# A planned attention-and-MLP kernel: landing times of the inputs, order of the waits, and thresholds per half block

## The chip, the cores and the metric

The kernel runs on one core of one Trainium2 chip. The core has five engines that work at the same time: TensorE (PE in the profile; its weight loads are shown apart as PEld), VectorE (DVE), ScalarE (ACT), GpSimd (POOL) and SyncE (SP), which here only issues transfers. Data lie in SBUF (128 partitions), matrix products in PSUM (8 banks of 128 x 512 float32), inputs and the output in HBM. The metric is the device time of one execution in microseconds (us), the median of several runs, lower is better.

## The reference, cut to what matters

S = 2048 rows, D = 640, H = 32 heads of Dh = 20, F = 1536. There is one key head and one value head for all 32 query heads.

```python
xn = layernorm(x)                       # over D, eps 1e-5
q = (xn @ wq) as (H, S, Dh); k = xn @ wk; v = xn @ wv      # k, v: (S, Dh)
p = softmax(q @ k.T * Dh ** -0.5)       # 32 x 2048 x 2048
a = concat_h(p @ v) @ wo                # (S, D)
h = relu(xn @ w1 + b1) ** 2             # (S, F)
out = x + a + (h @ w2 + b2)
```

All inputs are bfloat16. The 32 x 2048 x 2048 exponentials are most of the work outside TensorE.

## The kernel before, in words

**Blocks, tiles, units.** The queries are cut in 4 chunks of 512 (`QC`), the heads in 8 groups of 4 (`G`), which makes 32 *blocks*. A block goes over 16 key *tiles* of 128 keys. A tile has 4 *units*, one per head: a 128 x 512 piece of scores. The first two blocks run interleaved, four key tiles of each at a time, as the keys become ready.

**Two ways to the exponential.** PE computes two to four units at once, one per group of 32 array rows (`S_QK`, `qk_ins`, L1100); such a *batch* writes up to four PSUM banks. Most units go to ACT, two or three per instruction (`S_EXP`, L1280), which writes bfloat16 exponentials into a ring `PT`. The tiles called D (`S_D`, `dtiles`) go to DVE instead: `S_P1` (L1377) makes from each unit an integer whose bits are a coarse exponential, and three *phases* with added offsets (`S_PH` on DVE, L1398, or in pieces on POOL, `S_PHP`, L1460) refine it. A D tile costs PE four groups of products with the values instead of one (`PVblk`, L1567: itself and three phases). So work can be moved between ACT on one side and DVE, POOL and PE on the other, tile by tile.

**The rest.** `u_KT`, `u_V` and `u_QP` make keys, values and queries from the normalised and transposed input (L732, L791); `u_FFN` (L732, then L888 on DVE and a square on POOL, L896) and `u_OUT`, `u_PA`, `u_PB`, `u_P1`, `u_PX`, `u_PF` make the MLP and the output. They are queued as `units` by a block position at which each may start (`FAT`, `FSTEP` for the MLP) and are taken up by `S_MISC`, and at the start by two more such streams, between the attention batches.

**The planner.** No order is written by hand. `Sched.run` simulates the five engines with a fixed duration for each request; of the requests that can start at the same time on an engine it takes that with the smallest priority number (batches 0, P1 2, PV 1 or 0.8, phases 4, keys 1.5, values 2). Thresholds looked up by block, `plan(name)` at L1078, decide how many units a batch takes, when a D tile is opened, which bank a side job takes and so on. What comes out is one fixed instruction list per engine, executed in order. A mistaken duration therefore costs nothing in the simulation, but on the chip it leaves an engine standing at an instruction whose input is late, with later ones behind it.

**The start.** SP issues `x` in five parts (`x_dma`: row tiles 0-1, 2-3, 4-7, 8-11, 12-15) with `wq` after the third; ACT issues `wk` and `wv`. The planner believes in the landing times `xland` and those in the `dma` calls (L556 to L569). DVE computes the statistics of a row tile (`stats`, L634, L636), ACT 1/sqrt for four row tiles at once (`rst`, L644, L648), then a row tile is normalised (`xnorm`, L662 on DVE or POOL; row tile 3 on ACT, L664 after L653). Row tiles 0 to 3 are transposed on PE (L721) and copied out (`evac_te`, L676, L677); row tiles 4 to 15 are transposed by DMAs on the SP queue (`turn`, L682), about 1.3 us of issue each. Before that PE runs 22 warm-up products (L604) and four filler groups (L1497).

**Waits.** `resolve` finds for each operation the semaphores it must wait on, one counter per engine and one per transfer chain; `emit` asks for them one after the other before the operation. In the program as built, the one asked for first is carried by the operation's own first instruction; all others become wait instructions in front of it in the engine's queue. Before the change the order is that in which the dependencies were collected:

```python
            for s_, v_ in wd.values():
                e.wait_ge(s_, v_)
```

## Time and profile before

| | |
|---|---|
| median of 3 runs (lowest, highest) | 708.11 us (707.29, 708.21) |
| the profiled execution | 707.32 us, span 705.5 us |
| PE, DVE, ACT, POOL busy | 687.5, 667.7, 680.1, 426.3 us |
| first and last exponential on ACT | start 14.91 us, end 691.2 us |
| exponentials on ACT | 607 of two units, 82 of three |
| granted TensorE clock | 1.0 throughout |

The span is the time from the first to the last instruction; 1.8 us lie around it. PE, DVE and ACT are each busy for about 95% or more, so a shortage on one of them is hidden from the totals: the profile must be read by stretches, and by what ended each idle time. "A <- B" in the list of waits says that A's engine stood idle until B was done.

### The profile page before, as it was taken

To read this page: it belongs to the slowest core of one execution; us is meant where nothing else is said; L and a number is where in the kernel's file an instruction comes from. 1 tells how busy PE (TensorE), PEld (TensorE's weight loads), DVE (VectorE), ACT (ScalarE), POOL (GpSimd) and SP (SyncE) were. 2 spreads that over 40 slices of the span, in tenths; PEclk is the share of its full clock that TensorE was granted. 3 is DMA by queue.
4 is the path that set the end of the run, shared out by engine and by line. 5 is a ranking of instruction groups with operands and counts; after the bars stand their busy time and mean duration, and the time that the engine had idled before them with its cause. 6 is when DMAs were issued, how large, how long until landed. Compare 5 with 4: busy or idle time off the path is not lost.

```text
span 705.5 us, 23364 instructions
## 1 busy us (share of the span) xinstructions
PE 687.5 (97%) x9874; PEld 221.9 (31%) x9874; DVE 667.7 (95%) x1145; ACT 680.1 (96%) x708; POOL 426.3 (60%) x696
## 2 busy tenths in 40 slices
PE   8899999999999999999999999999999999999997
PEld 4232222222223333332223333333222333333335
DVE  6978999999999999999999999999999999999974
ACT  5999999999999999999999999999999999999991
POOL 2547667767665666666766666666676656566400
PEclk9999999999999999999999999999999999999999
DMA  6476111011100111111100121111110101111101
GB/s 199 67 189 184 37 21 30 14 21 29 26 17 17 35 38 31 45 22 38 34 14 14 25 49 41 26 39 32 30 26 18 26 20 41 26 34 39 35 2 40
DMA packets 37955, 29.47 MB, mean 42 GB/s; under 512 B 20218, under 2 KB 33499, under 8 KB 37851
## 3 DMA queue, kind: packets, MB, share of 16 engines
q1 hardware_dynamic: 36539, 27.92, 16.6%
q8 instruction: 79, 1.29, 0.8%
q10 hardware_dynamic: 1312, 0.05, 0.1%
q14 instruction: 25, 0.20, 0.1%
HBM read 10.87 MB, written 2.62 MB: 19 GB/s over the span
## 4 chain that ended last, share of the span: by engine, by line
PE 66%; DVE 29%; DMA 2%; issue 1%; ACT 1%; POOL 1%; SPq 0%; DVEq 0%
PE ps L1567 24%; PE ps L1100 22%; PE ps L732 20%; DVE pbx L1377 15%; DVE pbx L1398 9%; DVE hT_tmp L888 2%; DMA pbx<-in_A_x_dram 1%; ACT PT L1280 1%; DMA xnT<-big 1%; DVE big L662 1%; POOL pbx L1460 0%; DVE stats L634 0%; DVE Tn L1612 0%; DVE out_sb L943 0%; DVE qpk L843 0%
## 5 line engine op out<-in xcount | busy, mean ns | idle before, releaser
L1280 ACT ACTIVATE PT<-ps 128x1024 bf16<-128x1024 f32 (+1 forms) x689 | 672.7, 1097 | 3.8 <-PE ps L1100 3.3
L1460 POOL TENSOR_SCALAR pbx<-pbx 128x576 int16<-128x576 uint16 (+13 forms) x518 | 317.8, 635 | 176.4 <-DVE pbx L1398 169.7
L1377 DVE TENSOR_SCALAR pbx<-ps 128x512 int16<-128x512 f32 x576 | 381.6, 689 | 12.8 <-PE ps L1100 11.5
L1100 PE MATMUL ps<-qT,kT 20*128 20x512 bf16 x2048 | 268.7, 384 | 5.4 <-DVE pbx L1377 1.8
L1398 DVE TENSOR_SCALAR pbx<-pbx 128x2048 int16<-128x2048 int16 x308 | 212.7, 710 | 0.4
L1567 PE MATMUL ps<-pbx,vp 128*32 128x512 bf16 x1764 | 162.4, 383 | 1.8 <-DVE pbx L1398 1.4
L1100 PEld LDWEIGHTS ps<-qT,kT 20*128 20x128 bf16 x2048 | 68.5, 91 | 262.4 <-ACT PT L1280 189.7
L1567 PE MATMUL ps<-PT,vx 128*32 128x512 bf16 x1460 | 142.3, 384 | 1.8 <-ACT PT L1280 1.5
L732 PE MATMUL ps<-w_sb,big 128*32 128x320 bf16 x1536 | 82.1, 302 | 0.0
L732 PE MATMUL ps<-xnT,w_sb 128*32 128x512 bf16 x960 | 78.1, 383 | 0.1
L896 POOL TENSOR_TENSOR big<-hT_tmp 128x288 bf16<-128x288 bf16 (+5 forms) x88 | 56.1, 654 | 27.0 <-DVE pbx L1398 27.0
L1567 PEld LDWEIGHTS ps<-pbx,vp 128*32 128x32 bf16 x1764 | 43.5, 95 | 51.7 <-issue 34.4
L1567 PE MATMUL ps<-pbx,vx 128*32 128x512 bf16 x588 | 57.9, 384 | 1.6 <-DVE pbx L1377 0.9
L1567 PEld LDWEIGHTS ps<-PT,vx 128*32 128x32 bf16 x1460 | 37.6, 94 | 49.5 <-issue 37.6
L1628 POOL TENSOR_TENSOR OTs<-Tn,Rb 128x224 bf16<-128x224 f32 (+5 forms) x42 | 32.8, 782 | 20.3 <-DVE pbx L1398 20.3
L732 PEld LDWEIGHTS ps<-w_sb,big 128*32 128x32 bf16 x1536 | 32.6, 95 | 29.9 <-issue 22.2
L888 DVE TENSOR_SCALAR hT_tmp<-ps,b1col 128x512 bf16<-128x512 f32 x48 | 35.4, 737 | 0.7 <-PE ps L732 0.4
L732 PE MATMUL ps<-wo_p,OTp 120*32 120x320 bf16 (+1 forms) x640 | 34.2, 302 | 0.1
L732 PE MATMUL ps<-xnT,wq_sb 128*32 128x512 bf16 (+2 forms) x435 | 33.8, 373 | 0.0
L732 PEld LDWEIGHTS ps<-xnT,w_sb 128*32 128x32 bf16 x960 | 19.2, 94 | 26.9 <-issue 20.2
L1567 PEld LDWEIGHTS ps<-pbx,vx 128*32 128x32 bf16 x588 | 15.3, 94 | 19.9 <-issue 10.9
L1612 DVE COPY Tn<-ps 128x512 f32<-128x512 f32 x29 | 19.6, 677 | 0.2 <-PE ps L1567 0.2
(75 smaller groups left out, 181.3 us busy)
## 6 DMA issues: line engine op xcount, KB each, us to landing
Rb<-Rr SPq DMA_DIRECT2D x29, 256.0 KB
w_sb<-in_B_w_dram SPq DMA_DIRECT2D x2, 1920.0 KB
xres<-in_A_x_dram SPq DMA_DIRECT2D x16, 160.0 KB, 3.0
out_dram<-out_sb SPq DMA_DIRECT2D x16, 160.0 KB
qT<-qpk SPq DMA_DIRECT2D x105, 20.0 KB
pbx<-in_A_x_dram SPq DMA_DIRECT2D x3, 640.0 KB
OTp<-OTs SPq DMA_DIRECT2D x96, 20.0 KB
wq_sb<-in_A_wq_dram SPq DMA_DIRECT2D x1, 800.0 KB
```

Of the source, the lines that this page charges most:

```text
L662: fn = lambda e: e.tensor_scalar(out=xn_sb[:, st, :], in0=x_sb[:, st, :], scalar1=mean, scalar2=rstd[:, st:st + 1], op0=ALU.subtract, op1= ...
L732: return lambda e: e.matmul(ps[32 * j:32 * j + m, b_[0], 0:n], Lj, R, start=first, stop=last, tile_position=(0, 32 * j))
L888: v = yield Req(("dve", 658.0, 742.0, [lambda e: e.tensor_scalar(out=hT_tmp[:, k, :], in0=ps[:, b_[0], :], scalar1=b1col[:, f:f + 1], scal ...
L896: w = yield from pieces(512, 139.0, 1.7, lambda c0, c1: (lambda e: e.tensor_tensor(out=h2T[:, qc % 2, f, c0:c1], in0=hT_tmp[:, k, c0:c1], ...
L1100: ins.append(lambda e, i=i, b=b, t=t, h=h: e.matmul(ps[:, i, :], kT[32 * h:32 * h + DH, t * 128:(t + 1) * 128], qT[32 * h:32 * h + DH, b % ...
L1280: op = yield Req(("act", d_, d_ + 107.0, [lambda e, slot=slot, n=n, src=src: e.activation(out=PT[:, slot:slot + n, :], in_=ps[:, src, :], ...
L1377: return Req(("dve", d_, d_ + 82.0, [lambda e: e.tensor_scalar(out=PB[:, k, hsl, :], in0=ps[:, bk:bk + np_, :], scalar1=OFFS, scalar2=0.0, ...
L1398: return Req(("dve", 600.0, 684.0, [lambda e: e.tensor_scalar(out=PB[:, k, :, :], in0=PB[:, s, :, :], scalar1=PH_D[j], scalar2=None, op0=A ...
L1460: return lambda e: e.tensor_scalar(out=PB[:, k, :, :].rearrange("p h n -> p (h n)")[:, c0:c1], in0=PBU[:, s, :, :].rearrange("p h n -> p ( ...
L1567: ins = [(lambda e, h=h, first=first, last=last: e.matmul(ps[32 * h:32 * h + 32, bk, :], lhs, rhs[h], start=first, stop=last, tile_positio ...
L1612: v = yield Req(("dve", 600.0, 682.0, [lambda e: e.tensor_copy(out=Tn[:, tb, :], in_=ps[:, pvb, :])]), (lambda: None if oldt() is None els ...
L1628: w = yield from pieces(512, 138.0, 2.14, lambda c0, c1: (lambda e: e.tensor_tensor(out=dst[:, c0:c1], in0=Tn[:, tb, c0:c1], in1=Rb[:, a, ...
```

## The change

Four things are changed; no operation is added to or taken from the computation as such, but the planner's result, and so the whole order, may come out different.

1. **Landing times.** `xland` and the times of `wq`, `wk`, `wv` are set to other values. Row tiles 4-7 of `x`, for example, are now taken to land at 8.7 us instead of 6.7.
2. **Priorities at the start.** The projections of keys and values for chunks 1 to 3 get priority 0.9 instead of 1.5 and 2, which places them before ordinary PV groups (1); the copy of the values out of PSUM gets 14 for these chunks.
3. **Waits.** The semaphores of an operation are sorted by the planned completion of what they wait for, latest first. The latest therefore rides on the operation's own instruction, and the earlier ones are asked for in front of it.
4. **Thresholds.** The table `PLAN` has a row per half block (64) instead of one per block (32); four constants become columns of it (`give`, `await_`, `miscw`, `php`), and many values are different. The start positions of the MLP groups are changed: chunks 2 and 3 may start one block earlier (12 and 20 instead of 13 and 21) with a step of 0.36 instead of 0.33.

Against the row of the same block before, 58 of the 64 rows differ in at least one of the thirteen columns: 38 in `hungw`, 29 in `lead`, 27 in `ringhi`, 13 in `await_` (150 ns instead of 60 in 11 of them, 0 in 2), 9 in `miscw`, 8 in `give`, 6 in `php`.

```diff
-FAT = (1.0, 4.8, 13.0, 21.0)
-FSTEP = (0.3, 0.34, 0.33, 0.33)
+FAT = (1.2, 4.6, 12.0, 20.0)
+FSTEP = (0.28, 0.36, 0.36, 0.36)
...
+VPR, KPR, VEPR = 0.9, 0.9, 14.0
...
-GIVE = 3
...
+PSEG = 2
-PLAN_KEYS = ('lead', 'hungw', 'dstarv', 'clt', 'broken', 'p1tol', 'ringhi', 'miscr', 'mshift')
+PLAN_KEYS = ('lead', 'hungw', 'dstarv', 'clt', 'broken', 'p1tol', 'ringhi', 'miscr', 'mshift', 'give', 'await_', 'miscw', 'php')
...
-    (650.0, 3000.0, 600.0, 6000.0, 300.0, 900.0, 12, 2, 0.0),
-    (650.0, 3500.0, 600.0, 4500.0, 0.0, 900.0, 12, 2, 0.0),
+    (580.0, 3500.0, 600.0, 6000.0, 300.0, 900.0, 12, 2, 0.0, 3, 60.0, 300.0, 4.0),
+    (580.0, 3500.0, 300.0, 6000.0, 0.0, 900.0, 15, 2, 0.0, 3, 60.0, 300.0, 4.0),
+    (650.0, 4000.0, 600.0, 6000.0, 300.0, 900.0, 12, 2, 0.0, 3, 60.0, 300.0, 4.0),
+    (650.0, 3500.0, 600.0, 6000.0, 300.0, 900.0, 12, 2, 0.0, 3, 60.0, 600.0, 4.0),
...
-                    wd[d.sem.name] = (d.sem, d.val)
-            for s_, v_ in wd.values():
+                    wd[d.sem.name] = (d.sem, d.val, d.done)
+            for s_, v_, _ in sorted(wd.values(), key=lambda w: -w[2]):
                 e.wait_ge(s_, v_)
...
-        xland = [3700.0, 4600.0, 6700.0, 11000.0, 12900.0]
+        xland = [4000.0, 4850.0, 8700.0, 12000.0, 15000.0]
...
-        dma("sp", "wq", lambda e: e.dma_start(wq_sb[:], A_wq.rearrange("(dt p) n -> p dt n", p=128)), [], 8900.0)
+        dma("sp", "wq", lambda e: e.dma_start(wq_sb[:], A_wq.rearrange("(dt p) n -> p dt n", p=128)), [], 9800.0)
-        dma("act", "wk", lambda e: e.dma_start(wk_c[:], A_wk.rearrange("(dt p) d -> p dt d", p=128)), (lambda: get("tab")), 5000.0)
-        dma("act", "wv", lambda e: e.dma_start(wv_c[:], A_wv.rearrange("(dt p) d -> p dt d", p=128)), (lambda: get("tab")), 5500.0)
+        dma("act", "wk", lambda e: e.dma_start(wk_c[:], A_wk.rearrange("(dt p) d -> p dt d", p=128)), (lambda: get("tab")), 6300.0)
+        dma("act", "wv", lambda e: e.dma_start(wv_c[:], A_wv.rearrange("(dt p) d -> p dt d", p=128)), (lambda: get("tab")), 11000.0)
...
-            v0 = yield Req(("dve", 150.0, 230.0, [...]), [v], 10 + 4 * c, f"VE{c}")
+            v0 = yield Req(("dve", 150.0, 230.0, [...]), [v], 10 + 4 * c if c == 0 else VEPR, f"VE{c}")
...
-            return PLAN[min(NBLK - 1, int(pos()))][name]
+            return PLAN[min(NBLK * PSEG - 1, int(pos() * PSEG))][name]
...
-                    nd_ok = min(GIVE - (nd[0] - nd[1]), DMAXR)
+                    nd_ok = min(plan("give") - (nd[0] - nd[1]), DMAXR)
...
-                    free = [x for x in pool if freeat(x) <= t + AWAIT]
+                    free = [x for x in pool if freeat(x) <= t + plan("await_")]
...
-            return (min(fb, key=apart), sorted(freeat(x) for x in fb)[n] - MISCW) if len(fb) > n else None
+            return (min(fb, key=apart), sorted(freeat(x) for x in fb)[n] - plan("miscw")) if len(fb) > n else None
...
-... [acc[-1]] + pbres[k].last, 4 if left_ns(b) > URGN else 0.8, "PH", port=True)
+... [acc[-1]] + pbres[k].last, plan("php") if left_ns(b) > URGN else 0.8, "PH", port=True)
...
-            U(-3 + 0.1 * c + 0.05, f"KT{c}", ..., lambda b_, c=c: u_KT(c, b_, 1.5))
-            U(-3 + 0.1 * c + 0.06, f"V{c}", ..., lambda b_, c=c: u_V(c, b_, 2))
+            U(-3 + 0.1 * c + 0.05, f"KT{c}", ..., lambda b_, c=c: u_KT(c, b_, KPR))
+            U(-3 + 0.1 * c + 0.06, f"V{c}", ..., lambda b_, c=c: u_V(c, b_, VPR))
```

## The prediction

> **What bounds the kernel now.** I read the totals of the page, then the windows by stage, then what was waited for, then the first 15 us engine by engine. The totals say that three engines are full together:

> ```profile
> span 705.5 us, 23364 instructions
> PE 687.5 (97%) x9874; PEld 221.9 (31%) x9874; DVE 667.7 (95%) x1145; ACT 680.1 (96%) x708; POOL 426.3 (60%) x696
> ```

> The windows (PE, PEld, DVE, ACT and POOL busy) say which of them gives way where:

> ```profile
> 66.00:220.00 154.00, 148.09 (x1935) 42.62 (x1939) 153.46 (x253) 153.53 (x154) 104.22 (x157) 1.00 0.13 27
> 220.00:690.00 470.00, 467.98 (x6840) 149.80 (x6842) 454.06 (x757) 469.20 (x485) 291.05 (x480) 1.00 0.13 30
> ...
> 41.00:60.00 19.00, 18.46 (x242) 5.46 (x242) 13.48 (x23) 17.99 (x20) 9.48 (x15) 1.00 0.86 250
> 690.00:705.00 15.00, 11.62 (x336) 8.52 (x327) 6.78 (x18) 1.23 (x2) 0.00 (x0) 1.00 0.14 47
> ```

> From 66 to 220 us DVE and ACT have under 0.6 us of idle time and PE has 5.9; from 220 to 690 PE and ACT are full. The tail after the last exponential is a stream of PE products, 10 us long. What is left to gain is the first 66 us, short stalls, and the number of operations. The first input stall is a segment of the chain that ends last (its piece in the first 20 us), and then appears on DVE, ACT and PE:

> ```profile
> 1.82 6.92 DMA pbx<-in_A_x_dram
> ...
> 8.77 0.89 DVE stats L634 x2
> ...
> 9.75 0.92 ACT big L664
> ```
> ```profile
> 7.21 0.20 ACT L648 ACTIVATE rstd<-vtmp 128x4 f32<-128x4 f32 x1
> 9.75 0.92 ACT L664 ACTIVATE big<-pbx,nmr,rstd 128x640 bf16<-128x640 bf16 x1 [2.33 <-DVE nmr L653]
> ...
> 14.91 1.02 ACT L1280 ACTIVATE PT<-ps 128x1024 bf16<-128x1024 f32 x1 [0.57 <-PE ps L1100]
> ```
> ```profile
> 8.24 1.05 PE L1497 MATMUL ps<-hT_tmp,ones_bf 128*32 128x512 bf16 x16
> 10.12 0.45 PE L721 MATMUL ps<-ident,big 128*128 128x128 bf16 x5 [0.84 <-DVE big L662]
> ...
> 12.64 1.26 PE L732 MATMUL ps<-xnT,wq_sb 128*20 128x256 bf16 x40
> ```

> The reader should see that 1/sqrt is ready at 7.41 us, but DVE, in its fixed order, first takes the statistics of row tile 4, whose input lands at 8.74; nothing of row tiles 0 to 3 is normalised until 9.57. Last, the list of waits between 66 and 690 us (total, times, longest):

> ```profile
> PEld ps L1100 <- DVE pbx L1377: 12.1, 32, 0.4
> ...
> DVE pbx L1377 <- PE ps L1100: 6.8, 22, 0.8
> ```

> **Part A, landing times.** The semaphore records of the trace end at 4.07, 4.94, 8.74, 13.35 and 14.99 us for the five parts of x, 9.89 for wk, 11.44 for wq and 12.57 for wv. With 8.7 us for part three, the planner has the four normalisations (DVE starts 0.36 apart) ready at 7.4 and the statistics not before 8.8, so it turns their order round. The DVE gap of 1.81 us (6.96 to 8.77) is then used. The way to the first exponential gains less: PE is busy with warm-up and fillers until 9.29, so the first transposition moves from 10.12 to about 9.3 (0.83); its copies no longer queue behind L664 on ACT, so the first keys move from 12.09 to about 10.7, after wk; the queries move from 12.64 to no earlier than 11.44, where wq lands. From the queries on the chain is the same. The gain is between 0.83 and 1.2 us; I take 1.1, nearest to the wq row. The floor is 0, if the start is paid back later (a rival). The transfers are issued as before, in the same order, so SP pays nothing; the transposing DMAs move with their row tiles. The later figures for wk, wv and wq hold nothing up: keys and queries came after them anyway, and V starts at 14.81.

> **Part B, order of the waits.** I set each two-semaphore batch beside what released it in the trace's records. Where the later release had been asked for second, and is thus a wait instruction of its own, the batch starts 0.147 us after it ended, in 37 cases between 60 and 680 us, nearly always the same; where it had been asked for first, as little as 0.056 to 0.064. So 0.087 us is paid 37 times, 3.2 us of PE. Ten of these lie before 220 us, where PE has room. After 220, what a stall cost beyond the usual spacing (0.32 us from a batch's predecessor to it) is often less than 0.087, on average 0.06: 27 x 0.06 = 1.6 us. I take 1.3 and keep 0 and 3.2. Two-semaphore waits on DVE had the latest first in nearly all cases; POOL has some that turn round, and waited 155 us for DVE phases anyway, so nothing there; if that cover went, 15 x 0.09 = 1.3 us. What is queued behind a waiting batch is PE's PV and MLP groups, and ACT waits for it only when its two pending batches are used up. It can cost something where the planned latest is not the real one: in 44 of 448 two-semaphore batches, 0.087 each, 3.8 us if all of those were stalled, but only 9 of the 61 late ones were.

> [...]

> **Part C, priorities of keys and values.** Chunk 2's keys take from 37.95 to 40.1 on PE, five groups between batches and PV; then DVE copies them (0.75 at 40.61) and ACT stands idle for 0.93 us; 0.55 and 0.23 more at 25.6 and 29.1 hang on chunk 1. Groups of 0.22 us in a row would need 1.1 instead of 2.15 us. Of the 1.7 us of ACT idle time at most the first 0.93 is PE's order; the 0.55 is a PE stall on a transposing DMA. The work put back is PV, whose results nothing needs then. DVE has 5.5 us idle between 41 and 60. A D tile costs DVE 4 x 0.598 + 2.1 x 0.602 = 3.65 us (start to start, 2.1 of three phases on DVE: 308 for 147 tiles) and relieves ACT of 4 x 0.4525 = 1.81; so 1 us of DVE time is worth (1/3.65) / (1/3.65 + 1/1.81) = 0.33 us of time. Bounds 0 and 1.7 + 1.8 = 3.5; I take 0.5, half of the 0.93, since the DVE copy stays. VEPR places the value copies later on DVE: 0.15 each, with PV behind them; nothing.

> **Part D, thresholds per half block, and the MLP's starts.** These do no work themselves; they change which bank or batch is taken. From 66 to 690 DVE idles 16.5 us in the windows above, 6.7 of them in the last 8 us, where no D tile is left to make; of the other 9.8, 6.8 are waits for batches: x 0.33 = 2.2 us if all of it went. The other coin is PE: a batch costs 0.321 + 0.321 - 0.216 = 0.43 us (to it, from it, less what two neighbouring groups are apart anyway), and there are 689 (607 + 82 exponentials). A wider `await_` (150 ns in 11 half blocks) lets a unit join whose bank is free 90 ns later, and DVE's waits are mostly 0.1 to 0.4 us. Moving MLP groups a block forward moves 0.66 us of DVE each and changes no sum. Ends: 10 batches less or more, -4.3 to +4.3. I take -0.8, about a third of the DVE row's 2.2.

> **Sum.** 1.1 + 1.3 + 0.5 + 0.8 = 3.7 off the profiled 707.32 gives 703.6. That execution lies 0.8 below the median 708.11 and near the lowest of the three, so for a median I add half: 704.0. 0.2% is 1.4 us, about what a measurement of this kernel can tell from no change.

> **Rivals.** (1) The new plan makes more batches. The bound after 220 us is PE, which cannot hide 0.43 us each; the gains A to C of 2.9 us are used up at 7 more than 689, and 15 more cost 6.5 us: 708.1 - 2.9 + 6.5 = 711.7, slower from 11 on. For it: 58 of 64 rows differ, and `give` 2 or `hungw` 2600 in single half blocks make narrower batches. Against: in each column most rows hold the value that was the commonest before (`lead` 650 in 41 of 64, `give` 3 in 56). 22 in 100. (2) The start's gain is lost again at the keys of chunks 2 and 3: ACT comes 1.1 us earlier and waits 1.1 longer at 40.9, because the statistics of row tiles 8 to 15 and twelve transposing DMAs of 1.3 us on SP stand before them. Then C goes too, D comes out at nothing, and 708.1 - 1.3 = 706.8, no change. For it: that wait exists. Against: DVE itself gains the same 1.1 us. 12 in 100. (3) Ten batches fewer, or DVE's idle time in the first 66 us filled: 704.0 - 3.5 = 700.5. For it: 2.97 units per batch of four possible ones. Against: POOL and banks limit D. 24 in 100.

> **Numbers.** The forecast (702 to 706.5) has 42 in 100, rivals 22, 12 and 24. Faster by over 0.2%: 42 + 24 = 66; within: 12; slower: 22. The range leaves out 1 in 10 on each side: from 699.0, below rival 3, to 710.0, inside rival 1.

> **What would show it.** A: L662 starts by 7.7 us instead of 9.63, the first exponential at 13.8. B: no batch starts 0.147 us after its release. C: the 0.93 us before the exponential at 41.85 shrinks. D: count the exponentials and batches, and PE's busy time from 220 on. I am wrong if the number of batches or of D tiles moves by more than ten, or if the start moves and the tail does not.

## The result, and the profile after

The changed kernel is slower by about 1%: 715.53 us (median of 6 executions, 713.20 to 718.72) against 707.96 us for the kernel before beside it, ratio 1.0114 with a 95% interval of 1.0082 to 1.0145. I had forecast 704.0 with a range of 699 to 710. The profiled execution took 714.10 us, 712.3 of them the span. Between executions of one kernel the time here goes with the granted TensorE clock, a mean of 0.971 to 0.981 over the changed kernel's six executions and 1.000 in the profiled one before (one of the six executions before took 725.66 us, its clock is not on record, and the ratio leaves it out); so the clock is given with the times below.

The page of the changed kernel, totals and the row of the granted clock in 40 slices (tenths of full speed):

```profile
PE 696.2 (98%) x9882; PEld 220.6 (31%) x9882; DVE 665.8 (93%) x1144; ACT 679.5 (95%) x704; POOL 419.8 (59%) x670
...
PEclk9997599999999999999999999999999999999999
```

DVE and ACT do what they did before (667.7 and 680.1), PE seems to do 8.7 us more. The clock row says why: in the fourth and fifth slice it isn't full. The windows of the stages shown for the kernel before (PE, PEld, DVE, ACT and POOL busy, then the clock) say where the time went:

```profile
66.00:220.00 154.00, 152.24 (x1831) 40.09 (x1827) 145.09 (x238) 146.62 (x152) 101.36 (x153) 0.93 0.14 31
220.00:690.00 470.00, 468.95 (x6960) 150.98 (x6957) 459.49 (x771) 469.77 (x480) 290.11 (x464) 1.00 0.13 30
```

From 66 to 220 us ACT is busy 146.6 of 154 us where it was busy 153.5, at a clock of 0.93. From 220 us on nothing is lost. Following the 2048 score products of L1131 (L1100 before) gives the same: the 64th starts 1.8 us later than before, the 128th 6.8, the 192nd 14.8 (99.2 against 84.4), the 256th 14.3, the 2040th 12.1. The loss is made between 25 and 99 us; then some of it comes back, and the stretch behind the 2040th is shorter (15.1 us to the end of the span, before 20.5).

The windows around the two places, three microseconds each:

```profile
24.00:27.00 3.00, 1.71 (x17) 0.48 (x14) 3.00 (x11) 3.00 (x6) 0.00 (x0) 1.00 0.62 120
27.00:30.00 3.00, 2.58 (x32) 0.97 (x33) 0.32 (x2) 0.36 (x1) 0.70 (x1) 0.50 0.27 55
...
60.00:63.00 3.00, 0.42 (x3) 0.13 (x3) 0.00 (x0) 0.00 (x0) 0.00 (x0) 0.69 0.13 33
63.00:66.00 3.00, 3.00 (x25) 0.57 (x22) 2.23 (x4) 2.20 (x3) 0.17 (x1) 0.50 0.12 28
...
81.00:84.00 3.00, 3.00 (x29) 0.48 (x21) 1.71 (x3) 2.02 (x3) 1.58 (x3) 0.50 0.24 48
```

Two times PE goes idle, and two times the clock is half from then on. By the clock's records it is half from 27.00 for 3.41 us and from 61.13 for 27.31 us, eight times 3.41. From 63 us on in the second stretch PE is busy 3.00 of every 3.00 us and does 24 to 32 matmuls in them (45 and 48 in windows at full clock of the runs below), while DVE and ACT, nearly full in the kernel before, fall to about two thirds. The timeline of the same kernel has the gaps, and what is late (duration, then engine and operation, then in brackets the idle time before it and what ended it):

```profile
7.44 0.80 DVE L693 TENSOR_SCALAR big<-pbx,mv,rstd 128x640 bf16<-128x640 bf16 x2
...
16.87 2.66 POOL L693 TENSOR_SCALAR big<-pbx,mv,rstd 128x640 bf16<-128x640 bf16 x1 [0.97 <-ACT rstd L679]
19.56 6.40 SPq L713 DMA_TRANSPOSE xnT<-big  x4
27.42 2.31 PE L763 MATMUL ps<-xnT,wk_c 128*20 128x512 bf16 x20 [1.71 <-ACT PT L1311]
...
47.39 6.14 SPq L1066 DMA_DIRECT2D wo_p<-in_A_wo_dram  x4
...
55.36 4.62 SPq L892 DMA_DIRECT2D qT<-qpk  x6
...
62.58 0.61 PE L1131 MATMUL ps<-qT,kT 20*128 20x512 bf16 x3 [3.74 <-DMA qT<-qpk]
```

The first gap, 1.71 us. The planner now gives the normalisation of row tile 4 (`XN4`) to POOL, by `alts = [("dve", 400.0, 440.0, [fn]), ("pool", 880.0, 1000.0, [fn])]`; on POOL, beside DVE's work, it takes 2.66 us (0.45 on DVE in the same run). Four transposing DMAs stand behind it on SP in their order, 6.40 us in all, so the last is issued by 25.96, lands at 27.33 by its semaphore, and the keys of chunk 1 start at 27.42. The view puts the wait down to ACT, whose exponential was over at 25.36: the later release was the transposing DMA.

The second gap, 3.74 us. SP issues w1, w2 and nine loads of wo ahead of the queries of block 2. The planner counts 60 ns for each of those issues (`dma(..., issue=60.0)`); here they take from 46.20 to 55.32, 9.1 us, most of it one wo load that stands 5.0 us behind the two 1.9 MB loads. The kernel before has the same loads ahead, but everything on SP lies earlier, since its transposing DMAs began at 17.45: the queries of block 2 were issued from 53.53, had landed by 60.15, and its first batch of block 2 came at 60.82, with 0.7 us to spare. In the changed kernel they are issued from 55.36 and land at 62.45, 2.3 us later, and the new plan has PE at that batch by 58.84, 2.0 us earlier. Both together make the gap.

The waits that the prediction showed, in the changed kernel between 66 and 690 us:

```profile
PEld ps L1131 <- DVE pbx L1408: 45.8, 114, 1.0
...
DVE pbx L1408 <- PE ps L1131: 13.7, 32, 1.8
```

DVE's waits for batches have doubled (6.8 before): 5.9 us lie between 66 and 90, nearly all of it at half clock, and 7.8 behind it. The first row comes with the order of the waits, which the first experiment takes alone.

### The profile page after: what moved, and what is told of

Its sections match the earlier page's. It is cut to its first block, busy times and chain, and to the rows that moved or that the text cites. A ratio compares the mean times of both kernels' runs of the same rounds, so it can differ in the third digit from the quotient of the medians.

```text
span 712.3 us, 23357 instructions
## 1 busy us (share of the span) xinstructions
PE 696.2 (98%) x9882; PEld 220.6 (31%) x9882; DVE 665.8 (93%) x1144; ACT 679.5 (95%) x704; POOL 419.8 (59%) x670
## 3 DMA queue, kind: packets, MB, share of 16 engines
q1 hardware_dynamic: 36539, 27.92, 16.5%
## 4 chain that ended last, share of the span: by engine, by line
PE 70%; ACT 16%; DVE 11%; DMA 1%; POOL 1%; issue 1%; SPq 0%; DVEq 0%; POOLq 0%
PE ps L1598 25%; PE ps L1131 22%; PE ps L763 21%; ACT PT L1311 16%; DVE pbx L1408 6%; DVE pbx L1429 3%; PE ps L635 1%; DVE hT_tmp L919 1%; DMA qT<-qpk 1%; POOL big L693 0%; DMA dn<-Tn 0%; DVE qpk L874 0%; DVE Tn L1643 0%; PE ps L1527 0%; SPq L892 0%
## 5 line engine op out<-in xcount | busy, mean ns | idle before, releaser
L1491 POOL TENSOR_SCALAR pbx<-pbx 128x576 int16<-128x576 uint16 (+15 forms) x487 | 309.8, 655 | 184.4 <-DVE pbx L1429 165.2
L1408 DVE TENSOR_SCALAR pbx<-ps 128x512 int16<-128x512 f32 (+1 forms) x575 | 381.2, 691 | 24.7 <-PE ps L1131 23.2
L1131 PE MATMUL ps<-qT,kT 20*128 20x512 bf16 x2048 | 270.8, 390 | 7.4 <-DMA qT<-qpk 3.7
L1429 DVE TENSOR_SCALAR pbx<-pbx 128x2048 int16<-128x2048 int16 x309 | 210.4, 702 | 0.8
L1131 PEld LDWEIGHTS ps<-qT,kT 20*128 20x128 bf16 x2048 | 66.9, 91 | 271.5 <-ACT PT L1311 180.0
L763 PE MATMUL ps<-xnT,w_sb 128*32 128x512 bf16 x960 | 82.9, 399 | 0.6 <-DVE pbx L1408 0.2
L763 PE MATMUL ps<-w_sb,big 128*32 128x320 bf16 x1536 | 79.7, 302 | 0.0
L1659 POOL TENSOR_TENSOR OTs<-Tn,Rb 128x224 bf16<-128x224 f32 (+5 forms) x43 | 32.9, 767 | 16.5 <-DVE pbx L1429 16.5
L1598 PEld LDWEIGHTS ps<-pbx,vx 128*32 128x32 bf16 x588 | 15.2, 95 | 20.5 <-issue 12.7
```

Source lines behind the costliest of these rows:

```text
L763: return lambda e: e.matmul(ps[32 * j:32 * j + m, b_[0], 0:n], Lj, R, start=first, stop=last, tile_position=(0, 32 * j))
L1131: ins.append(lambda e, i=i, b=b, t=t, h=h: e.matmul(ps[:, i, :], kT[32 * h:32 * h + DH, t * 128:(t + 1) * 128], qT[32 * h:32 * h + DH, b % ...
L1408: return Req(("dve", d_, d_ + 82.0, [lambda e: e.tensor_scalar(out=PB[:, k, hsl, :], in0=ps[:, bk:bk + np_, :], scalar1=OFFS, scalar2=0.0, ...
L1429: return Req(("dve", 600.0, 684.0, [lambda e: e.tensor_scalar(out=PB[:, k, :, :], in0=PB[:, s, :, :], scalar1=PH_D[j], scalar2=None, op0=A ...
L1491: return lambda e: e.tensor_scalar(out=PB[:, k, :, :].rearrange("p h n -> p (h n)")[:, c0:c1], in0=PBU[:, s, :, :].rearrange("p h n -> p ( ...
L1598: ins = [(lambda e, h=h, first=first, last=last: e.matmul(ps[32 * h:32 * h + 32, bk, :], lhs, rhs[h], start=first, stop=last, tile_positio ...
```

## The experiments

My theory after this, G: behind two gaps of PE (1.71 and 3.74 us) the granted clock falls to half, the half clock (3.41 and 27.31 us) is the loss, and the rest of the change is a gain. The texts written ahead of the runs say that the clock gate closes where the granted clock falls from 1.00 to 0.50. The rivals: P, the new plan is worse in itself and the clock only goes along with it; S, the stall alone is the loss. All times below are medians with the lowest and highest, then the mean granted clock. The sets were taken on two chips and at different times, and the kernel before moved by 1.2 us between them; a difference of that size between two sets says nothing.

| kernel | us | clock | ratio to the kernel before (95%) |
|---|---|---|---|
| before | 707.2 to 708.4 in five sets | 0.995 to 1.000; 0.982 or 0.983 in 5 of 62 executions (715.6 to 717.8 us) | |
| changed | 715.53 (713.2 to 718.7) | 0.971 to 0.981 | 1.0114 (1.0082 to 1.0145) |
| before, sorted waits alone | 704.44 (704.1 to 704.9) | 0.999 to 1.000 | 0.9932 (0.9906 to 0.9958) |
| before, landing times alone | 735.61 (727.2 to 743.4) | 0.955 to 0.988 | |
| before, sorted waits and thresholds | 721.03 (720.3 to 721.5) | 0.989 to 0.992 | 1.0164 (1.0098 to 1.0230) |
| changed, both causes moved | 704.69 (701.4 to 712.7) | 0.980 to 0.998 | 0.9950 (0.9921 to 0.9980) |
| the same, denominators first | 697.75 (697.3 to 703.1) | 0.992 to 1.000 | 0.9861 (0.9787 to 0.9935) |
| the same, with fillers | 698.42 (697.4 to 699.0) | 1.000 | 0.9856 (0.9779 to 0.9932) |

### One part alone: the order of the waits

```diff
-                    wd[d.sem.name] = (d.sem, d.val)
-            for s_, v_ in wd.values():
+                    wd[d.sem.name] = (d.sem, d.val, d.done)
+            for s_, v_, _ in sorted(wd.values(), key=lambda w: -w[2]):
```

> The kernel before with one part of the change alone: the semaphores of an instruction are asked for latest first. All lists stay. My prediction's step B: 1.3 us off, 706 to 707 (0 to 3.2 us off), and starts 0.147 us after a release become starts 0.06 us after it on TensorE. Rival: the engine stands at a batch anyway for something else, 707.5 to 708.5. Rival: the order by planned time is wrong where it matters and costs, above 708.5.

704.44 us, 4.0 off by the medians, and 2.8 between the two profiled executions, both at full clock (spans of 705.5 and 702.7). Part of the 4.0 is the clock, which is 0.999 or more in all eight executions of this kernel and below that in 8 of 19 of the kernel before: against the other 11 (median 708.0) the gain is 3.6. The bounds that I had given were 0 and 3.2. The counts moved as foreseen. Of the two-semaphore batches from 100 to 680 us that came more than 0.32 us behind the product before them, 40 started 0.14 to 0.15 us after the release in the kernel before (of 50), and 10 (of 33) here, with 18 at 0.06 to 0.08. The waits between 66 and 690 us, in the kernel before and in this one:

```profile
PEld ps L1100 <- issue: 47.9, 133, 0.5
```
```profile
PEld ps L1100 <- DVE pbx L1377: 39.1, 103, 0.8
...
PEld ps L1100 <- issue: 19.0, 58, 0.4
```

Time that was put down to the sequencer (47.9 us) now shows as waiting for DVE (12.1 before, 39.1 here): the wait that ends last is part of the instruction and not a step ahead of it. The gain is 0.4 us at the first score product, which the order of the waits need not have made (the first product moves by more than that between executions of the same lists), 0.6 by the 256th, 1.4 by the 1024th, 2.2 by the 1536th and 2.7 by the last: it comes in small pieces, most of them behind 100 us.

### One part alone: the landing times, and the thresholds

```diff
-        xland = [3700.0, 4600.0, 6700.0, 11000.0, 12900.0]
+        xland = [4000.0, 4850.0, 8700.0, 12000.0, 15000.0]
...
```

> The kernel before with one part of the change alone, the landing times of the inputs; the planner plans everything anew from them, with the old thresholds and priorities and the old order of the waits, and puts the normalisations of row tiles 4 and 12 on POOL; it makes 706 batches instead of 689. My prediction's step A taken alone would be 1.1 us off (707). Theory G: with row tile 4 on POOL the gap before chunk 1's keys comes from this part, with a half clock behind it; and 17 batches more at 0.43 us cost 7 us: 716 to 728. If the gap doesn't appear, it comes from the priorities: 712 to 716.

735.61 us (727.2 to 743.4). Windows of this kernel:

```profile
18.00:21.00 3.00, 2.29 (x27) 0.71 (x27) 2.79 (x8) 3.00 (x4) 2.70 (x4) 0.81 0.06 13
21.00:24.00 3.00, 3.00 (x24) 0.48 (x20) 2.90 (x7) 2.57 (x3) 0.00 (x0) 0.50 1.17 95
...
220.00:690.00 470.00, 466.48 (x6778) 148.64 (x6778) 436.03 (x723) 466.63 (x487) 254.21 (x398) 1.00 0.13 30
```

POOL takes 2.65 us over row tile 4 as in the changed kernel, and the last of its four transposing DMAs lands at 27.25; so the cause of the first gap comes with the landing times. The gap itself isn't seen here. The clock is half from 19.87 for 23.89 us, before the keys of chunk 1 are due, and on the slowed PE their turn comes at 28.74, when they have nothing to wait for. In the 3.41 us ahead of the fall of the clock PE waits 0.83 and 0.28 us for exponentials of the first tiles: a third place at which the clock fell. From 43.76 on the clock is full, so the second gap does not come from here. And at full clock, from 220 us on, DVE does 436 us of work instead of 454: with this start the old thresholds meet other moments and make a worse plan, of 140 D tiles and 706 batches where the kernel before has 147 and 689. The reverse, thresholds without landing times and priorities, on the kernel with sorted waits:

```diff
-FAT = (1.0, 4.8, 13.0, 21.0)
-FSTEP = (0.3, 0.34, 0.33, 0.33)
+FAT = (1.2, 4.6, 12.0, 20.0)
+FSTEP = (0.28, 0.36, 0.36, 0.36)
...
+PSEG = 2
...
-            return PLAN[min(NBLK - 1, int(pos()))][name]
+            return PLAN[min(NBLK * PSEG - 1, int(pos() * PSEG))][name]
```

> The kernel before with sorted waits (704.44) and the thresholds of the change (the table by half blocks, the four values moved into it, the MLP's starts), but with the old landing times and the old priorities of keys and values. My prediction's step D taken alone would be 0.8 us off, with bounds of 4.3 on both sides: 703.6 (700 to 709). Theory T (the thresholds fit one plan only, the one that comes from the new landing times and priorities; with another start they fall on other batches): 695 batches instead of 689, more idle time between batches, 708 to 716. Rival (they are better values in themselves): 698 to 704.

721.03 us, 16.6 more than with sorted waits alone, and above what I expected even by theory T. Its list of waits from 10 to 120 us, and a window:

```profile
PE ps L1131 <- DMA qT<-qpk: 2.4, 1, 2.4
```
```profile
220.00:690.00 470.00, 462.35 (x6812) 149.65 (x6811) 434.80 (x725) 465.44 (x479) 278.10 (x435) 1.00 0.13 30
```

The thresholds bring the gap before block 2 (2.4 us, then half clock from 61.58 for 10.24 us), and again DVE loses 18 us of work against sorted waits alone (452.7), with 141 D tiles and 695 batches. By an estimate, the gap and the half clock, at the prices found below (0.32 to 0.45), are 6 to 7 of the 16.6 us; the rest goes with the plan. So the thresholds aren't better values by themselves: with the old start they make a worse plan.

### Gaps filled, opened and moved in the changed kernel

First, zeros into the gap: 16 groups of four products ahead of the stalled batch.

```diff
+        pe[at].pre = [(lambda e, h=h: e.matmul(ps[32 * h:32 * h + 32, bk_, :], zeros32[:, :],
+                       kT[:, 0:512], start=False, stop=False, ...)) for _ in range(16) for h in range(HPG)]
```

> The changed kernel with 16 groups of four products of zeros put into TensorE's list just ahead of the stalled batch of block 2. They have nothing to wait for, so they run inside the 3.74 us that TensorE stands at 58.8 to 62.6 us; the late query transfer, the plan and every other list stay. Theory G (the loss is the clock: the gap at 58.8 closes the clock gate, and 27 us at half clock cost 27 x 0.5 x the share that TensorE limits, about 8 to 12 us): the half clock between 61 and 88 us is gone, the stall itself stays (3 to 4 us), total 704 to 707.5. Rival P (the loss is the new plan: its orders and batches are worse, and the half clock comes with it): the clock stays full and the total is still above 711. Rival S (the loss is the stall of 3.7 us alone): nothing gained but the clock's own share, total 713 to 716.

716.01 us (709.5 to 722.4, clock 0.972 to 0.997): the number was missed, the mechanism was half seen.

```profile
63.10 3.63 PE L1855 MATMUL ps<-kT,zeros 128*32 128x512 bf16 x64
67.70 0.39 PE L1134 MATMUL ps<-qT,kT 20*128 20x512 bf16 x3 [0.97 <-DMA qT<-qpk]
```

Behind the filled gap the clock stays full (1.00 from 63 to 87 us). But in this execution it was half for 17.07 us behind the first gap instead of 3.41 (26.14 to 43.20), and for 10.24 us more behind a new gap, a wait of DVE for a transfer of the denominators at 84 us. The one execution with a clock of 0.997 took 709.5, still more than the forecast of 704 to 707.5; the stalls themselves were still there, but what makes up the rest isn't known. Next, the loads of w2 and wo (`w2`, `wo0` to `wo7`, `wob`, `wop`) put behind the query transfers, with every other list as it was:

```diff
...
+            k_ = next(i for i, o in enumerate(lst) if o.dma == "Q5_1") + 1
+            lst[k_:k_] = mvd_
```

> The changed kernel with one thing moved: the loads of w2 and of wo are issued on SP's queue behind the query transfers of block 2 instead of ahead of them; all other engines' lists are the same. Theory G with the query transfer as the cause of the gap: Q2_0 is issued by about 52 us instead of 55.4, the first batch of block 2 starts within 1 us of the PV before it, no half clock between 61 and 88 us, total 702 to 705.5. If another transfer is late in its place, the stall moves and the half clock stays: 712 to 716. If the loss is the new plan's orders: above 711 although the stall is gone. If the weights now come late for the first output projection (before 150 us), a stall there: 706 to 712.

717.61 us, clock 0.979 in all four. Behind the first gap (1.79 us here) the clock is half for 17.07 us. The gap before block 2 is gone, and another has come in its place, by the list of waits from 15 to 100 us:

```profile
DVE rd L1648 <- DMA dn<-Tn: 10.6, 2, 9.1
...
PE ps L1131 <- DVE pbx L1408: 8.4, 1, 8.4
```

The load `wop` waits for w2 to land, and while it does SP issues nothing: the denominators of block 0 were ready at 69.50 and issued at 76.56. Behind PE's stall of 8.4 us the clock is half for 13.65 us. I had moved a wait to a place with more behind it. Third, the zeros behind the stalled batch instead of ahead of it:

> The changed kernel with the same 16 groups of products of zeros put right behind the first batch of block 2 instead of ahead of it: the gap stays as it was, and TensorE has 64 products more to do while the clock is half (16 x 0.43 = 6.8 us). [...]

```profile
66.00:69.00 3.00, 3.00 (x40) 1.20 (x36) 0.00 (x0) 0.00 (x0) 0.00 (x0) 0.65 0.30 68
69.00:72.00 3.00, 3.00 (x45) 0.99 (x41) 1.54 (x3) 1.57 (x2) 0.07 (x1) 1.00 0.66 154
```

The clock is half for 6.83 us (61.30 to 68.13) instead of 27.31: it is full again within the stretch of zeros, where in the changed kernel the usual mix went on at half clock. This is one profiled execution. The time is 720.08 (713.9 to 727.2), no better than the changed kernel's; in the profiled execution the clock had also been half from 27.17 for 3.41 us, and was again from 88.61 for 13.65 us, behind a wait of DVE for denominators.

### The gap by itself, in the kernel before

Both of these are the kernel before with sorted waits, with one query transfer (`Q2_0`) issued later; the second also has 24 groups of zeros ahead of the stalled batch.

```diff
+        for lst in (sc.lists["sp"], sc.order):
+            mvd_ = next(o for o in lst if o.dma == "Q2_0")
+            lst.remove(mvd_)
+            lst.insert(next(i for i, o in enumerate(lst) if o.dma == "Q3_1") + 1, mvd_)
```

> The test of the cause by itself, on the kernel before with sorted waits (704.44, clock 1.0 in all eight executions): one transfer of block 2's queries is issued behind those of block 3 and the first of the next set, so that it lands at about 66 us instead of 58 and TensorE stands some 5 us before the first batch of block 2 (60.4). Nothing else is changed. Theory G: the gap alone closes the clock gate, as in the changed kernel, for 20 to 31 us; 704.4 + 5 for the gap + 4 to 8 for the half clock, 713 to 718, clock 0.976 to 0.985. Rival (the half clock needs the new plan's mix of work): clock 0.995 or more and 706 to 710.

> The same, with 24 groups of products of zeros (24 x 0.22 = 5.3 us) ahead of the stalled batch, so that TensorE has columns to do while it waits. Theory G: the clock stays full, and the gap alone is left: 704.4 + 4.5 to 6 = 709 to 710.5, clock 0.998. The difference of the two is the price of the half clock. Rival (columns of zeros don't count, or the gate goes by something else): as without them, 713 to 718.

715.91 us (715.1 to 721.1, clock 0.978 to 0.990) without the zeros and 710.46 (708.9 to 719.3) with them, on a plan of 704.44. Eight of the ten executions with zeros have a clock of 0.999 or 1.000 and take 708.9 to 710.7; two have 0.985 and take 718.7 and 719.3, and where the clock fell in these isn't known. Windows of the first, then a line of the second's timeline and its window:

```profile
63.00:66.00 3.00, 0.21 (x3) 0.14 (x3) 0.00 (x0) 0.00 (x0) 1.55 (x4) 0.62 0.32 61
66.00:69.00 3.00, 3.00 (x25) 0.53 (x22) 2.04 (x3) 1.64 (x2) 0.73 (x2) 0.50 0.14 31
```
```profile
61.17 5.35 PE L1824 MATMUL ps<-kT,zeros 128*32 128x512 bf16 x96
```
```profile
66.00:69.00 3.00, 3.00 (x48) 0.78 (x40) 2.10 (x4) 2.05 (x3) 0.67 (x1) 1.00 0.12 27
```

Without the new plan, a gap of 5.07 us alone makes the clock half for 17.07 us (63.74 to 80.81). The gap costs 710.46 - 704.44 = 6.0 us (from two sets, so to about a microsecond), and the half clock 715.91 - 710.46 = 5.4 us, 0.32 us for each of its 17.07. That settles it against S, and shows that the clock needs no new plan to fall: the plan wasn't touched, and zeros that do no work, and only give PE something to do in the gap, take the second half of the loss away. P, for the changed kernel's own loss, is met by the next runs.

### Both causes taken away

In the lists of the changed kernel, after its planning: `XN4` and `XN15` go from POOL to the same place in DVE's order, and the loads of w2 and wo behind the queries of block 6 (`wop` behind block 3's broadcast; all are used from 229 us on).

```diff
+        for n_ in ("XN4", "XN15"):
...
+            o_.eng = "dve"
...
+        for ns_, at_ in ((late_, "Q6_2"), ({"wop"}, "dc3")):
```

> Only the first of the two: the normalisations of row tiles 4 and 15 on DVE, the loads left ahead of the query transfers. Theory G: TensorE's gap at 25.7 us falls from 1.71 us to under 0.7 and the clock stays full there; the gap before block 2 stays (3 to 5 us) and the clock falls behind it as before, 711 to 716. If the second gap was only long because the first had delayed it: no half clock, 702 to 706.

The normalisations alone: 711.18 us (710.2 to 713.4). The keys of chunk 1 start at 25.05 without a wait and the clock stays full until 59.71; then the gap before block 2 comes (3.83 us), and half clock for 23.89 us.

> Only the second: the loads of w2 and wo behind block 6's query transfers, the normalisation of row tile 4 left on POOL. Theory G: the gap at 25.7 us stays, and the half clock behind it (3.4 us or, as with the two kernels of the first runs, 17 us); no gap before block 2 and no 8 us wait for the denominators, which in the run with the loads directly behind block 2's query transfers came from the load of wo that waits for w2 on SP's queue; 704 to 712, the low end if the clock is half for one window, the high end for five.

The loads alone: 710.52 us (704.6 to 718.3, clock 0.973 to 0.998). The first gap is there in the profiled execution too (1.67 us before the keys of chunk 1), and the clock stayed full behind it; it was half from 76.32 for 3.41 us, behind a wait of DVE for denominators (2.92 us).

> The changed kernel with the causes of both early gaps taken away and its plan otherwise kept, instruction for instruction: the normalisations of row tiles 4 and 15 go from POOL (2.66 us for row tile 4, beside DVE's work) to the same place in DVE's order, and the loads of w2 and wo, used from 229 us on, are issued behind the query transfers of block 6 instead of ahead of those of block 2 (9.1 us of SP). Theory G (two gaps on TensorE, and the half clock that follows them, are the whole loss; the rest of the change is a gain): keys of chunk 1 by 26 us, first batch of block 2 within 1 us of the product before it, no half clock but that before 7 us and after the end, spans 697 to 701, total 699 to 703, that is below the kernel before with sorted waits alone (704.44). Rival P (the new plan is worse in itself): clock full and total above 706. Rival N (with these gaps gone the next late thing, the denominators' transfers around 84 us, opens another gap and the clock falls again): 706 to 713.

Both: 704.69 us, in two groups. Six of twelve executions have a clock of 0.998 and take 701.36 to 702.67 us; the others have 0.980 to 0.990 and take 706.7 to 712.7. From the fastest to the slowest executions it is 11.2 us for 17.5 thousandths of mean clock; a thousandth is 1.4 us at half clock, so by this estimate each microsecond at half clock costs 0.45 us. Theory G holds for the first group. Rival N explains a part of the second: in the profiled execution (708.18 us) the clock is half behind the denominators, from 79.21 for 6.83 us, but also before that, from 21.18 for 10.24 us, with neither gap in front of it. Its windows there:

```profile
18.00:21.00 3.00, 1.88 (x23) 0.53 (x23) 3.00 (x10) 3.00 (x3) 0.00 (x0) 1.00 0.29 59
21.00:24.00 3.00, 2.57 (x22) 0.52 (x22) 2.91 (x7) 2.52 (x4) 0.00 (x0) 0.53 1.34 102
```

PE stands 0.83, 0.19 and 0.70 us for exponentials between 17.8 and 21.4; this is the third place, seen already with the landing times alone. The gap of rival N, in the timeline of SP and DVE:

```profile
71.60 0.57 SPq L1654 DMA_DIRECT2D Rb<-Rr  x1
72.84 0.54 SPq L1646 DMA_DIRECT2D dn<-Tn  x1
...
78.82 0.25 DVE L1648 RECIPROCAL rd<-dn 128x16 f32<-128x16 f32 x1 [2.96 <-DMA dn<-Tn]
```

The denominators of block 1 (8 KB) go out 1.2 us behind block 0's broadcast (256 KB) and land at 78.80, 5.4 us after their issue is through. What the broadcast feeds on POOL is done at 88.71 only. So the next kernels turn the two round:

```diff
+        for lst in (sc.lists["sp"], sc.order):
+            mvd_ = next(o for o in lst if o.dma == "dc0")
+            lst.remove(mvd_)
+            lst.insert(next(i for i, o in enumerate(lst) if o.dma == "da1") + 1, mvd_)
```

> The same without the fillers, that is with the denominators' transfer ahead of the broadcast alone. [...] Rival: the broadcast was not what held the transfer, and the wait stays: 701 to 709 as before.

> The changed kernel with both causes moved as in the run of that kind (clean 701.4, but 705 to 713 in half of its executions), and two things more: the transfer of block 1's denominators goes ahead of block 0's 256 KB broadcast on SP's queue (behind it, it landed 5.4 us after its issue, and DVE stood 2.96 us for it at 75.9), and eight filler groups of zeros go ahead of six batches between 18 and 27 us, where TensorE stands for 0.7 to 0.8 us each before a batch. Theory G: neither early gap is left, so no execution falls into the half clock: all between 698 and 702, clock 0.998 or more. If something else closes the gate in some executions, these come out at 705 and above again. If the fillers stand in the way of the batches: clean executions above 702.

697.75 us without fillers, three of four executions from 697.3 to 697.9, and 703.05 at a clock of 0.992; 698.42 with them, 697.4 to 699.0, all four at 1.000. Four executions each can't tell whether the fillers prevent what the one execution shows; in the others they cost about 0.7. DVE no longer waits for the denominators. From the page of the version without fillers (span 695.6 us), and a window:

```profile
PE 684.3 (98%) x9882; PEld 219.7 (32%) x9882; DVE 664.8 (96%) x1146; ACT 677.6 (97%) x704; POOL 412.9 (59%) x668
```
```profile
66.00:220.00 154.00, 151.55 (x1970) 42.87 (x1966) 152.42 (x252) 153.33 (x160) 106.93 (x165) 1.00 0.18 42
```

It is 1.4% faster than the kernel before and, by the medians, 17.8 us faster than the change as it was made, with the same instructions but for the engine of two normalisations. So the new plan isn't worse in itself, and P falls. Last, the same version with the old order of the waits:

> The changed kernel with the three moves (XN4 and XN15 to DVE, the late loads, block 1's denominators first; 697.5 clean), and the order of the waits as it was before the change. On the kernel before, asking for the latest semaphore first was worth 4.0 us (708.41 to 704.44). If it is worth the same here: 700.5 to 702 in clean executions. If the new plan has its latest semaphores first anyway: 697 to 699.

700.10 us (699.5 to 700.3): in the new plan the order of the waits is worth 2.4 us by the medians and by the spans of the profiled executions (698.0 and 695.6). The two were taken on two chips, and as shares of the kernel before beside each (0.9885 and 0.9867) it is 1.3.

## Why the prediction was wrong

**What bounds the kernel.** Three full engines from 66 us on is right. I showed the column of the granted clock, 1.00 in every window, and took it for a constant. In these runs it fell to 0.50 behind stalls of PE (for 27.31 us behind 3.74 us in the changed kernel, for 17.07 us behind 5.07 us in the kernel before with one transfer later), and none of my terms or rivals had it: a stall of PE was priced at its length.

**Part A.** The planner turned the order round as I said: L693 starts at 7.44 (by 7.7 forecast), the first exponential at 14.49 here and at 13.95 in the best version (13.8 forecast, 14.91 before). One execution can't tell this gain, since with the same lists that start moves by more than a microsecond: in the ten profiles of the new plan it lies from 13.51 to 15.00, mean 14.17, and in the four of the old from 14.53 to 15.40, mean 14.96, 0.8 earlier by the means. The step that failed is what stands behind: "SP pays nothing; the transposing DMAs move with their row tiles". With the new landing times the planner also picks POOL for row tile 4, 2.66 us for 0.45, and TE4 goes out at 19.56 instead of 17.45. The trace of before had the price: row tile 6 on POOL took 2.51 us. I priced the move by the tiles that come first and not by those whose engine may change. Taking row tile 4's normalisation (and row tile 15's) back to DVE, alone, makes the changed kernel 4.4 us faster (711.18).

**Part B.** The mechanism was right and the term too small: 1.3 taken, bounds 0 and 3.2; measured 2.8 (profiled) to 4.0 (medians) on the kernel before and 1.3 to 2.4 in the new plan. I had let the wait instruction cost nothing before 220 us and less than its 0.087 us elsewhere.

**Part C.** The 0.93 us before the exponential at 41.85 is gone: in the changed kernel ACT runs without a break from 35.64 to 45.3. (The 0.22 us for a group of four products, in this term and in D's, is the spacing in the trace of before where groups follow each other: 677.16, 677.39 and 677.61.) Its share in time was not measured alone.

**Part D.** "Moving MLP groups a block forward ... changes no sum" was not run by itself. The term for all of D was too small, and a price was missing from it. In the version without gaps, 212 PE instructions stand behind the last batch instead of 344; from the last batch to the end of the span it is 11.1 us, with sorted waits alone 16.3. That is 5.2 us where I had taken 0.8 for all of D; up to the last batch it is ahead by 1.8 more. That the MLP's new starts make this tail is not shown: the landing times alone, with the old starts, leave 136 instructions behind the last batch, and the thresholds with the old start 128. The same thresholds, though, put the first batch of block 2 where its queries had not landed; here lies the second failed step, 3.74 us and the half clock behind it. Taking the loads out of the way, alone, gives 710.52, 5.0 us less. I looked at batches and tiles (684 for 689, and 147 D tiles in both, well within the ten that I allowed) and not at what each moved batch waits for on SP.

**The sum.** My terms made 3.7 us off. Without the gaps the change is 10.2 us off (707.96 to 697.75). With them it is 7.6 on. As an estimate, the difference of 17.8 us is two gaps of 5.45 us together, and 30.7 us at half clock at 0.32 to 0.45 us each, 9.8 to 13.8: 15.3 to 19.3. Rival 1 would have cost 711.7, but by batches that were not made; rival 2 was near in place (a transposing DMA on SP late for the keys), with one chunk earlier and a price that knew no clock. That the start's gain is lost again at the keys of chunk 1 is what happened, at four times the price (4.4 us for 1.1).

## What to carry to other kernels

In a kernel like this a stall of PE isn't priced at its length: behind one of 3.74 us the granted clock was half for 27.31 us, though PE was busy again, and each of these cost 0.32 to 0.45 us by the estimates above. So ask of every moved batch which transfer it waits for and what stands ahead of that on its queue, with the durations of the trace and not of the plan; fill what can't be avoided, or, better, issue late what is used late. Thresholds that were fitted to one plan are not values that can be judged alone.

## What the runs showed of the hardware that I had not expected

PE's busy time alone doesn't tell the falls. The three microseconds from 18 to 21 us, with PE busy for 1.88 of them, stand ahead of a fall at 21.18 (both causes moved); with PE busy for 1.95 of them, no fall came before 27.17 (zeros behind the batch). Nor does it tell the returns: in the changed kernel the clock stayed half from 63 to 87 us, with PE busy 3.00 us of every 3.00 and 24 to 32 products in them. What makes the clock fall and return isn't shown. Shown is that zeros in the gap before block 2 left it full in both profiled executions with them (1.00 from 63 to 87 us in the changed kernel, from 57 to 93 us in the kernel before with sorted waits), and, in one execution, that it was full again at 68.13 within a dense stretch of zeros.

On one queue a small transfer came late behind a large one: 8 KB issued behind 256 KB landed 5.4 us after its issue was through (both causes moved), and in the version with the two turned round DVE used them without a wait at 70.76, 2.4 us after their issue was through. And an issue itself stood: in the changed kernel one wo load of 25 KB held SP for 5.0 us right behind two loads of 1.9 MB, the seven others of its size 0.32 to 0.33 us each.
